# Gated attention and a max-out MLP on one core: other release points for the next sequence's loads of v

## The chip, the cores and the metric

The kernel runs on one core of one Trainium2 chip. The metric is the device time of one execution in microseconds (us), the median of several executions. Times inside an execution come from a profile of one execution and are counted from the start of its span.

## What is computed

There are eight sequences of 3072 tokens. u and v have 256 columns, z has 64, all float32.

```python
scores = scale * np.matmul(z, z.transpose(0, 2, 1))      # scale = 1/3072
attn = np.maximum(scores, 0.0) ** 2
x = u * np.matmul(attn, v)                               # then reshaped to 24576 x 256
h1, h2 = x @ w1, x @ w2                                  # 256 -> 1024
out = np.maximum(h1, h2) @ w_out                         # 1024 -> 256
```

The kernel computes in bfloat16 with float32 accumulation.

## The kernel before

**Steps.** A sequence is cut into six groups of 512 tokens (`G` = 4 blocks of 128 tokens, `NG` = 6 groups). A step computes the result of one group of queries; there are 48 steps, and step n belongs to sequence n // 6. The scores are symmetric, so a tile of scores of groups (i, j) is computed once, and its transpose is made by a DMA (`turn`, L564 for the diagonal blocks and `do_turn`, L449, for whole tiles, which land in tiles named aT). The product with v and the last layer are done by a scheme of seven products in place of eight of 2 x 2 blocks. This needs sums of blocks: VectorE makes sums of v's blocks once per pair of groups (`add_fold`, L366; the tile is called lf; the additions carry the lines L290 and L293), and sums of score blocks for each step (`add_sums`, L613; the tile es).

**Phases of a step.** From the fourth step on, TensorE goes through a step in four passes over the six groups: Xa and Xb (three products for each half) and Ya and Yb (four products for each half). Between and inside them stand the first layer of an earlier step (da, db), the last layer of a still earlier step (o), and the scores of steps to come. `QUIET` (L1483) holds the first job of Xb, of Ya and of Yb of each step: the beginnings of the second, third and fourth pass.

**Loads.** GpSimd issues all loads of u, v and z, since they cast float32 to bfloat16 (`load`, L107). Its queue is in order. A load of v (`add_v`, L344) brings one group, 512 tokens of 256 columns, 256 KB as bfloat16; the six groups come in the order 1, 2, 3, 4, 5, 0, and two of them in turn fill one tile and are folded together. The tile pool has six such tiles, so two sequences fit. Loads of the first sequence go out at the start. Any other load is timed: it waits for the newest matmul that stands ahead of it in the program (L109), so that it does not go out too early. u (`add_u`, L1497) is loaded one group for each step; z (`add_z`, L1525) is loaded for the next sequence in the third step, and its two transposes (zT) come after that. SyncE issues all transposes and stores, in order.

**Where a load is placed.** The place is given as a step of the sequence before and a time in us within that step by a plan of TensorE's work; `at_step` (L1479) finds the first job that the plan has at that time or later, and `quiet` (L1487) moves on to the next job of `QUIET`. For the sequences 2 to 7 (counted from 0) the loop at L1548 holds the list for v:

```python
            z_at, zT_at = (2, 9), (3, 4)
            v_at = [(3, 11), (3, 16), (4, 5), (4, 12), (5, 2), (5, 6)]
        add_z(b, quiet(at_step(b - 1, *z_at)), at_step(b - 1, *zT_at))
        for g, at in zip(v_order(b), v_at):
            add_v(b, g, quiet(at_step(b - 1, *at)))
```

Sequence 1 has a list of its own. u is placed at 4 us of a step, which `quiet` turns into the first job of Xb.

**The order of everything else.** The order on TensorE is written out beforehand (`pe_order`). A planner (`find_orders`, L1756) with costs of all jobs then decides the order on VectorE, ScalarE, SyncE and GpSimd, and which of ScalarE and VectorE does a job that either can do. A load's place enters this plan, and so do costs for DMAs. The orders are fixed in the program.

Of the kernel before, what the change touches and what calls it, by code (L numbers as in the profile page):

```python
# [11 lines left out]
def kernel(  # L12
# [306 lines left out]
    def v_order(b):  # L319
        return [1, 2, 3, 4, 5, 0] if b else list(range(NG))  # L320
# [23 lines left out]
    def add_v(b, g, at):  # L344
        first = v_pair(b, g)[1] == 0
        if first:
            buf(*v_key(b, g), lambda: vpool.tile([P, 2, G, D], bf16, name="v_sb"))

        def fetch(_):
            load(  # L350
                timed=at is not None,
                out=v_tile(b, g),
                in_=v[b].rearrange("(p t) d -> p t d", p=P)[:, ds(g * G, G), :],
            )

        job(
            ("v", b, g),
            {"POOL": 1300},
            fetch,
            new=v_key(b, g) if first else None,  # L360
            uses=[v_key(b, g)],
            after=list(at or ()) + ([] if first else [("v", b, v_order(b)[v_order(b).index(g) - 1])]),
            lag=8000,
        )
# [1114 lines left out]
    def at_step(b, s, us):  # L1479
        return pe_job_at(starts[NG * b + s] + us * 1000)  # L1480
# [6 lines left out]
    def quiet(at):  # L1487
        i = pe_order.index(at[0])
        if pe_at[i] < starts[LAG]:
            return at  # L1490
        found = [key for key in pe_order[i:] if key in QUIET]
        return found[:1] or at
# [32 lines left out]
    def add_z(b, at, turn_at):  # L1525
        def fetch(_):
            load(
                timed=True,
                out=z_sb_0[:, 1 : 1 + NSB, :],
                in_=z[b].rearrange("(p t) d -> p t d", p=P),  # L1530
            )

        def turn_z(_):
            seqs[b].zT = make_zT(z_sb_0)

        job(("z", b), {"POOL": 1800}, fetch, after=at, lag=7500)
        job(("zT", b), {"SP": 3500}, turn_z, deps=[("z", b)], after=turn_at, lag=3500)
# [10 lines left out]
    for b in range(1, B):  # L1548
        if b == 1:
            z_at, zT_at = (2, 6), (3, 2)  # L1550
            v_at = [(0, 8), (3, 12), (3, 16), (4, 4), (4, 8), (5, 4)]
        else:
            z_at, zT_at = (2, 9), (3, 4)
            v_at = [(3, 11), (3, 16), (4, 5), (4, 12), (5, 2), (5, 6)]
        add_z(b, quiet(at_step(b - 1, *z_at)), at_step(b - 1, *zT_at))
        for g, at in zip(v_order(b), v_at):
            add_v(b, g, quiet(at_step(b - 1, *at)))
# [422 lines left out]
```

## Time and profile before

| | us |
|---|---|
| runs shown | 908.16, 907.21, 898.59 |
| median | 907.21 |
| the profiled execution's own time | 907.36 |
| its span, first to last instruction | 905.6 |
| TensorE busy in the span | 887.9 |
| VectorE busy | 788.7 |
| ScalarE busy | 754.9 |
| GpSimd busy | 58.6 |
| median from issue to landing: v, u, a transpose to aT | 5.9, 5.4, 5.2 |

The span is 1.8 us shorter than the execution's own time. Busy time of an engine leaves out what its sequencer does (waits, issues of DMAs). A wait is put down to what ended it; "issue" means that the engine waited for nothing that the profile shows. "DMA share" is the time of all packets as a share of the 16 DMA engines' time; packets of several queues overlap, so that it can be over 1.

### The profile page before, as it was taken

The page shows a single profiled execution, that of the slowest core. Times are in us where ns is not written, and L with a number is a line of the kernel's source. Part 1 is how long each engine was busy: PE and PEld are TensorE (multiplying, and loading weights), DVE is VectorE, ACT ScalarE, POOL GpSimd, SP SyncE. Part 2 cuts the span into 40 slices and gives each one's busy share as a digit, 9 for nine tenths or more (in the row PEclk, how much of TensorE's full clock was granted, in tenths as well). Part 3 has the DMA queues.
Part 4 walks back from the last instruction along what each step waited for, and adds up shares of the span by engine and source line. Part 5 has one row for each costly group of instructions (what it writes and reads, how often), then busy time and mean ns, then how long its engine had stood idle before and what let it go on. Part 6 is the DMA issues. An engine that isn't in the chain of part 4 may idle for free.

```text
span 905.6 us, 37106 instructions
## 1 busy us (share of the span) xinstructions
PE 887.9 (98%) x16333; PEld 743.3 (82%) x16333; DVE 788.7 (87%) x1701; ACT 754.9 (83%) x946; POOL 58.6 (6%) x115
## 2 busy tenths in 40 slices
PE   8979999999999999999999989999999999999998
PEld 3349888988888888888888878888888898888885
DVE  6856888999999999999999889988999899989970
ACT  8846999789987899888997879977999789997635
POOL 3100000000000000001000000000000001000000
PEclk9989999999999999999999999999999999999999
DMA  9999999999999999999999999999999999999711
GB/s 164 188 136 178 173 183 158 188 155 180 172 166 151 171 184 156 162 175 188 156 159 171 186 151 150 166 173 165 184 149 182 164 190 160 158 172 159 124 61 70
DMA packets 382929, 146.64 MB, mean 162 GB/s; under 512 B 361264, under 2 KB 362928, under 8 KB 382768
## 3 DMA queue, kind: packets, MB, share of 16 engines
q1 hardware_dynamic: 366208, 114.54, 79.3%
q0 software_dynamic: 16560, 29.74, 23.4%
q8 instruction: 127, 2.08, 0.9%
q14 instruction: 34, 0.28, 0.1%
HBM read 59.77 MB, written 25.17 MB: 94 GB/s over the span
## 4 chain that ended last, share of the span: by engine, by line
PE 75%; DVE 12%; ACT 6%; DMA 3%; issue 3%; SPq 0%; POOL 0%; DVEq 0%; POOLq 0%
PE acc L87 38%; PE s_ps L87 37%; DVE es L290 2%; ACT g_sb L276 2%; DMA v_sb<-in_v_dram 2%; ACT a_sb L276 2%; DVE es L293 2%; DVE a_sb L293 1%; DVE e L290 1%; DVE xT L297 1%; DVE e L293 1%; DVE o_sb L293 1%; ACT a_sb L282 1%; DVE gs L293 1%; DMA z_sb<-in_z_dram 1%
## 5 line engine op out<-in xcount | busy, mean ns | idle before, releaser
L87 PEld LDWEIGHTS <-v_sb 64*128 64x128 bf16 (+1 forms) x4464 | 333.9, 94 | 68.3 <-issue 12.9
L276 ACT ACTIVATE a_sb<-s_ps 128x1024 bf16<-128x1024 f32 (+1 forms) x335 | 301.6, 944 | 36.3 <-PE s_ps L87 34.6
L87 PE MATMUL acc<-es,v_sb 64*128 64x256 bf16 x2160 | 278.5, 269 | 0.0
L87 PEld LDWEIGHTS <-lf 64*128 64x128 bf16 x3240 | 264.2, 94 | 17.2 <-POOLq L95 5.3
L87 PE MATMUL acc<-es,lf 64*128 64x256 bf16 x1080 | 246.6, 269 | 0.1
L87 PE MATMUL acc<-a_sb,lf 64*128 64x256 bf16 x1224 | 232.7, 269 | 0.0
L282 ACT ACTIVATE a_sb<-a_sb 128x1024 bf16<-128x1024 bf16 (+1 forms) x219 | 213.0, 993 | 2.3
L87 PE MATMUL s_ps<-xT,w_sb 64*128 64x512 bf16 (+1 forms) x1484 | 212.9, 376 | 0.1
L276 ACT ACTIVATE g_sb<-s_ps 128x1024 bf16<-128x1024 f32 x187 | 185.9, 1024 | 8.7 <-PE s_ps L87 7.2
L87 PE MATMUL acc<-aT,lf 64*128 64x256 bf16 x936 | 178.3, 269 | 0.9 <-issue 0.6
L87 PE MATMUL acc<-a_sb,v_sb 64*128 64x256 bf16 (+1 forms) x1344 | 142.4, 279 | 1.9 <-DMA a_sb<-a_sb 1.2
L87 PE MATMUL s_ps<-zT 64*128 64x512 bf16 (+2 forms) x774 | 120.2, 333 | 2.5 <-DVE o_sb L290 1.2
L290 DVE TENSOR_TENSOR es<-aT 128x1536 bf16<-128x1536 bf16 (+1 forms) x117 | 106.3, 930 | 0.0
L87 PEld LDWEIGHTS <-gs 64*128 64x128 bf16 x2688 | 98.7, 94 | 8.4
L87 PEld LDWEIGHTS <-g_sb 64*128 64x128 bf16 x2336 | 92.3, 94 | 11.9 <-POOLq L95 7.1
L87 PEld LDWEIGHTS <-w_sb 64*128 64x128 bf16 (+1 forms) x1488 | 79.5, 94 | 26.6 <-POOLq L95 1.0
L284 DVE TENSOR_TENSOR a_sb<-a_sb 128x1024 bf16<-128x1024 bf16 (+1 forms) x117 | 72.6, 625 | 23.7 <-ACT a_sb L276 23.5
L87 PE MATMUL acc<-aT,v_sb 64*128 64x256 bf16 x936 | 87.4, 270 | 3.5 <-DMA aT<-a_sb 3.5
L293 DVE TENSOR_TENSOR es<-a_sb 128x512 bf16<-128x512 bf16 x198 | 78.8, 418 | 6.7 <-PE acc L87 6.6
L87 PE MATMUL s_ps<-wf_sb,gs 64*128 64x128 bf16 x2016 | 80.8, 216 | 0.0
L87 PE MATMUL s_ps<-w_out_sb,g_sb 64*128 64x128 bf16 (+1 forms) x1664 | 79.7, 228 | 0.0
L290 DVE TENSOR_TENSOR es<-a_sb 128x1024 bf16<-128x1024 bf16 x108 | 72.0, 683 | 0.0
(87 smaller groups left out, 1079.5 us busy)
## 6 DMA issues: line engine op xcount, KB each, us to landing
out_dram<-o_sb SPq DMA_DIRECT2D x47, 512.0 KB, 4.7
v_sb<-in_v_dram POOLq DMA_DIRECT2D x48, 256.0 KB, 5.9
u_sb<-in_u_dram POOLq DMA_DIRECT2D x48, 256.0 KB, 5.4
aT<-a_sb SPq DMA_TRANSPOSE x228, 5.2
z_sb<-in_z_dram POOLq DMA_DIRECT2D x7, 384.0 KB, 6.8
w_sb<-in_moe_w_dram POOLq DMA_DIRECT2D x2, 512.0 KB, 7.6
uT<-u_sb SPq DMA_TRANSPOSE x48, 4.8
a_sb<-a_sb SPq DMA_TRANSPOSE x45, 5.3
```

The lines of the kernel that those rows point to most:

```text
L87: newest[0] = pin(nc.tensor.matmul(*args, **kw)).ins
L276: pin(nc.scalar.activation(out_ap, in_ap, AF.Relu))
L282: pin(nc.scalar.activation(ap, ap, AF.Square))
L284: pin(nc.vector.tensor_mul(ap, ap, ap))
L290: pin(nc.vector.tensor_add(*args))
L293: pin(nc.vector.tensor_sub(*args))
L297: nc.vector.scalar_tensor_tensor(out=out_ap, in0=in0, scalar=c2, in1=in1, op0=ALU.mult, op1=ALU.mult)
```

## The change

One line: for the sequences 2 to 7, the six loads of v get other places in the sequence before.

```diff
         else:
             z_at, zT_at = (2, 9), (3, 4)
-            v_at = [(3, 11), (3, 16), (4, 5), (4, 12), (5, 2), (5, 6)]
+            v_at = [(2, 13), (3, 9), (3, 13), (4, 9), (4, 13), (5, 9)]
         add_z(b, quiet(at_step(b - 1, *z_at)), at_step(b - 1, *zT_at))
         for g, at in zip(v_order(b), v_at):
             add_v(b, g, quiet(at_step(b - 1, *at)))
```

After `quiet`, the loads of v wait for these jobs of TensorE (steps counted from 0 within the sequence; u is loaded at the first job of Xb of each step, z at the first job of Ya of step 2):

| group | before | after |
|---|---|---|
| 1 | step 3, Yb | step 2, Yb |
| 2 | step 4, Xb | step 3, Ya |
| 3 | step 4, Xb | step 3, Yb |
| 4 | step 4, Yb | step 4, Ya |
| 5 | step 5, Xb | step 4, Yb |
| 0 | step 5, Ya | step 5, Ya |

The orders on TensorE, ScalarE and VectorE are the same in both programs. On GpSimd one place in each of the six sequences changes: group 1 comes ahead of the load of u that is issued in step 3. The loads of u issued in steps 4 and 5 keep their places behind groups 3 and 5. On SyncE two places in each of the six sequences change: during step 4 the transpose of u goes ahead of a store and of the transpose of a diagonal block, and during step 5 it and a store go ahead of the transpose of a tile of scores.

## The prediction

> **What bounds the kernel now.** I read the page first: its busy line, its forty slices and its DMA rows.
>
> ```profile
> span 905.6 us, 37106 instructions
> PE 887.9 (98%) x16333; PEld 743.3 (82%) x16333; DVE 788.7 (87%) x1701; ACT 754.9 (83%) x946; POOL 58.6 (6%) x115
> DMA  9999999999999999999999999999999999999711
> q0 software_dynamic: 16560, 29.74, 23.4%
> q8 instruction: 127, 2.08, 0.9%
> ```
>
> TensorE is busy for 98% of the span: 17.7 us are idle in all. The DMA engines are at 9 tenths or more in 37 slices of 40. So nothing that moves a load can win much unless a load now holds TensorE up, and any stretch with more loads in it may hurt. Next the windows of the six whole sequences whose loads the change moves (columns: stretch, its length, busy PE, PEld, DVE, ACT, POOL with counts, TensorE clock, DMA share, GB/s).
>
> ```profile
> 112.00:221.00 109.00, 108.84 (x2148) 94.74 (x2147) 98.27 (x211) 95.94 (x122) 6.37 (x12) 1.00 1.13 172
> 221.00:331.00 110.00, 107.63 (x2126) 93.63 (x2123) 101.16 (x221) 95.69 (x120) 6.90 (x13) 1.00 1.07 167
> 331.00:440.00 109.00, 108.80 (x2144) 94.48 (x2140) 101.95 (x222) 96.38 (x123) 6.90 (x13) 1.00 1.08 169
> 440.00:551.00 111.00, 107.45 (x2115) 93.75 (x2113) 101.10 (x220) 95.29 (x121) 6.90 (x13) 1.00 1.07 164
> ```
>
> Two sequences lose 2.37 us (110.00 − 107.63) and 3.55 us; the others, 551 to 769 us too, lose 0.2 each. The clock is 1.00 in all of them. TensorE's own waits from 112 to 770 us, in total, times, longest:
>
> ```profile
> PE s_ps L87 <- issue: 3.2, 2, 2.3
> PE s_ps L87 <- DVE o_sb L290: 1.2, 2, 0.6
> PE acc L87 <- DVE e L290: 0.6, 1, 0.6
> PE acc L87 <- issue: 0.6, 1, 0.6
> ```
>
> That is all there is to win: 5.6 us. None of it is a wait for a transposed tile or for v itself. I followed both kinds back.
>
> The waits for VectorE come from v. The chain of waits and VectorE's timeline have it: the last load of v of a sequence (group 0) lands late, the fold at L290 waits, and VectorE, busy without a break after that, is late for TensorE at 230.87 (0.62 us) and 243.57 (0.61 us), and at 462.22 (0.58 us).
>
> ```profile
> 221.37 6.84 DMA v_sb<-in_v_dram
> 440.93 5.94 DMA v_sb<-in_v_dram
> ```
> ```profile
> 228.34 0.42 DVE L290 TENSOR_TENSOR lf<-v_sb 128x512 bf16<-128x512 bf16 x1 [1.30 <-DMA v_sb<-in_v_dram]
> 446.99 0.43 DVE L290 TENSOR_TENSOR lf<-v_sb 128x512 bf16<-128x512 bf16 x1 [0.40 <-DMA v_sb<-in_v_dram]
> ```
>
> The waits for "issue" stand at 286.57 (0.98 us), 527.16 (0.60) and 542.87 (2.27). I read them as TensorE out of instructions: queue q8 moved 2.08 MB in 127 packets, 16.4 KB each, one for every 257 of PE's and PEld's 32,666 instructions. In the trace's packet records these three waits end 1.3 to 1.6 us after a q8 packet that began 12.2, 9.4 and 9.4 us behind the one before it, where the mean is 905.6/127 = 7.1. This is an inference. The timeline of GpSimd shows what was on the way just before the longest:
>
> ```profile
> 526.43 0.53 POOL L108 DMA_DIRECT2D v_sb<-in_v_dram  x1 [8.04 <-PE s_ps L87]
> 528.06 0.53 POOL L108 DMA_DIRECT2D v_sb<-in_v_dram  x1 [1.10 <-PE acc L87]
> 529.04 0.53 POOL L108 DMA_DIRECT2D u_sb<-in_u_dram  x1 [0.45 <-PE acc L87]
> 536.24 0.53 POOL L108 DMA_DIRECT2D v_sb<-in_v_dram  x1 [6.66 <-PE s_ps L87]
> ```
>
> Three loads within 2.6 us, then a fourth.
>
> **The change part by part.** Nothing is added or removed: 36 loads of v (six each for the third to the eighth sequence, groups in the order 1, 2, 3, 4, 5, 0) get other release points. Orders on TensorE, ScalarE and VectorE stay as they were; GpSimd's and SyncE's queues change. Each load waits for the newest matmul, so the new times are the ends of those matmuls in the trace of before. For the sequence loaded around 390 to 446 us (old → new): group 1 408.9 → 391.2; group 2 417.5 → 404.9; group 3 418.2 → 408.9; group 4 426.4 → 422.5; group 5 435.8 → 426.4; group 0 stays at 440.9. u, which has no load of v ahead of it for the same matmul any more, moves from 419.2 to 417.4 and from 436.7 to 435.8. z stays at 387.2.
>
> *Issue on GpSimd.* The same 0.53 us rows, on an engine 6% busy: nothing. Group 1 is now ahead of one u in the queue, but its matmul ends 8 us before that u's: no wait is inherited.
>
> *SyncE's queue.* Twice in each sequence a transpose of u moves ahead of a store and a transpose of scores; that blocks what stands behind it until u lands. Near 417 us u starts 1.8 us sooner, so its transpose can issue near 423 instead of 427.10; the store (issued at 423.73) hardly moves and the transpose of a diagonal block (420.89) goes some 3.6 us later, against 39 us until its first reader. Near 440 us a transpose goes from 439.64 to about 442.5; its tile is first touched again 28 us after it landed. Cost: nothing; the cover is these leads. Were they gone, the price would be the same 3 to 4 us on each.
>
> *Fold of the last pair.* Until now three loads (group 5, u, group 0) fall into the last 5 us before it, after the change two. Price of a load: q0's 23.4% of 905.6 us is 211.9 us for 29.74 MB, so 0.262 MB take 1.87 us of all engines. Group 0 lands up to 1.87 us sooner; VectorE waited 1.30 and 0.40. Both go. TensorE gets back 1.23 us, and of the 0.58 no more than the 0.40. Sum −1.6 (bounds 0 and −1.8).
>
> *The bunch of three.* Gone; loads come 4 to 9 us apart. The wait of 0.60 at 527 stays: it came with one load on the way, and group 3 takes group 1's old place. The 2.27 at 542.87 fell behind the bunch, but after the change groups 4 and 5 are near. I take −1.5, two thirds of it; the bounds are 0 and all three rows, −3.85.
>
> Here a page is weighed against these rows. The Trainium skill, "Runtime: NRT & Kernel Launch", section "Instruction fetch mechanics", says that instructions come in 16 KiB blocks of 256 and that this is mostly hidden. The size agrees (16.4 KB for 257 instructions); "hidden" would make these three waits something that no load changes, and this term zero.
>
> *z and group 1.* The third step gets a load more, 4 us behind z, where zT's transposes follow (396.56 to 401.35 on SyncE). The windows give a DMA share of 1.16 for 387 to 397 us, 1.33 for 397 to 407, against 1.00 for 417 to 427. Before the 0.98 us wait at 286.57 there was z alone (277 to 287 us: share 1.22). Group 1 can lengthen that, and start one in the other five sequences. Below: 0, since the other five show no wait there. Above: the largest row, 2.27, in each of six: +13.6. Nearest is the sequence that shows a wait: I take +0.8 in it (half of 2.27 − 0.98, and a little for the others).
>
> *Transposes behind it.* Everything on SyncE from 391 to 411 us shares its time with one load more, and the last transposes there with two: up to 2 × 1.87 = 3.7 us later. The tightest tile there, the fourth step's turned group 4, lands at 410.46 and TensorE reads it 4.19 us later (4.3 to 6.4 in the other sequences); zT has 6.4. Cost: nothing by 0.5 us; if all fails, about 1 us in each of six.
>
> Sum: −1.6 − 1.5 + 0.8 = −2.3. The profiled execution took 907.36 us (span 905.6 and 1.8 around it), 0.15 above the median of 907.21. 907.36 − 2.3 − 0.15 = 904.9.
>
> **The rivals.**
> *All stalls go.* If bunches caused every issue wait, the whole 5.6 us goes: 907.2 − 5.6 = 901.6. For it: the undisturbed sequences lose only 0.2 us, and one of the three runs took 898.59, so TensorE's work fits into that. Against: two of the three issue waits had one load beside them. Its range runs from 898 to 902, and lower only if the runs lose something that this execution doesn't show.
> *Loads don't reach the issue waits.* Only the fold's term is left: 907.2 − 1.6 = 905.6. For it: v's bunch stands in all six sequences and only one shows the long wait. This is what the page above, the Trainium skill's "Instruction fetch mechanics", would make of it.
> *Slower: group 1 behind z starves TensorE in every sequence.* Place: 391 to 407 us and its like. Price: 2.27 each, 13.6 − 1.6 = +12.0: 919.2. For it: the highest DMA shares, and the one wait there with z alone. Against: five of six showed none. It decides from (9.1 + 1.6)/6 = 1.8 us a sequence on; at 0.98 it is 911.5 and within 1%.
>
> **How the numbers follow.** A measurement can tell about 1% from no change here: 9.1 us, so 898.1 and 916.3. The forecast, 901 to 911, has 0.45; all stalls gone 0.27; loads without effect on issue 0.09; starved 0.19. Under 898.1 lies about half of the second case at most: 0.14. Over 916.3 the fourth: 0.19. Within: 0.67. The time is that of the forecast. The range leaves out the fourth case and takes in the second to its end: 897.5 to 912.
>
> **What would show it.** Right: no wait for DMA ahead of any fold at L290 in the third to eighth sequence; TensorE's waits for VectorE under 0.5 us; issue waits of 2 to 3 us in all, the larger ones 5 to 20 us behind z. Wrong: issue waits in most sequences, or TensorE waiting for aT in the fifth step; or a sum of issue waits that hasn't moved though the loads stand apart.

## The result, and the profile after

The changed kernel took 908.77 us (median of 20 executions, 903.49 to 918.14), the kernel before 904.07 (20 executions, 898.59 to 908.16). The ratio is 1.0049, with a 95% interval of 1.003 to 1.0068: slower by about 4.4 us, half of the 1% that the prediction took for no change, but clear of chance. Ratios here and below leave out the few slow executions (here the one of 918.14 us), and so differ a little from the quotient of the medians. The forecast was 904.9 and a gain of a quarter of a per cent: the direction is wrong. That the forecast lies within 4 us of the median is in part luck. It was counted down from 907.21, the median of three executions; counted from the 904.07 of twenty, the same sum gives 901.8.

The profiled execution after took 912.19 us. Its page, busy line first:

```profile
span 910.4 us, 37107 instructions
PE 889.9 (98%) x16333; PEld 744.7 (82%) x16333; DVE 788.6 (87%) x1701; ACT 754.7 (83%) x946; POOL 58.4 (6%) x115
```

The span is 4.8 us longer: TensorE is idle for 2.8 us more (20.5 in place of 17.7) and busy for 2.0 more. The work of VectorE and ScalarE is the same. The same windows as before (stretch, length, busy PE, PEld, DVE, ACT, POOL, clock, DMA share, GB/s):

```profile
112.00:221.00 109.00, 107.97 (x2124) 93.72 (x2121) 98.02 (x211) 95.54 (x121) 6.34 (x12) 1.00 1.08 170
221.00:331.00 110.00, 109.11 (x2158) 94.69 (x2154) 101.86 (x222) 96.31 (x122) 6.87 (x13) 1.00 1.08 169
331.00:440.00 109.00, 108.72 (x2146) 94.53 (x2142) 102.03 (x222) 96.51 (x122) 6.88 (x13) 1.00 1.08 170
440.00:551.00 111.00, 104.97 (x2056) 91.37 (x2054) 98.27 (x217) 92.30 (x116) 6.34 (x12) 1.00 1.16 159
...
660.00:769.00 109.00, 107.97 (x2125) 93.72 (x2123) 100.98 (x222) 95.35 (x121) 6.86 (x13) 1.00 1.08 169
```

The stretch from 440 to 551 us now loses 6.03 us (111.00 − 104.97), where it lost 3.55. The first, the second and the last lose about 1 each; the other two lose 0.3. In the second, 221 to 331 us, this is less than the 2.37 of before: the issue wait of 0.98 us that the prediction expected to grow is not there. TensorE's own waits from 112 to 770 us (in total, times, longest):

```profile
PE s_ps L87 <- issue: 4.6, 3, 2.1
PE acc L87 <- DMA aT<-a_sb: 1.5, 1, 1.5
PE acc L87 <- issue: 1.5, 3, 0.7
PE s_ps L87 <- ACT a_sb L282: 0.5, 1, 0.5
PE s_ps L87 <- DVE o_sb L290: 0.2, 1, 0.2
```

They sum to 8.3 us, where they were 5.6. The waits for VectorE have shrunk from 1.8 to 0.2; "issue" has grown from 3.8 to 6.1, and a wait for a turned tile (aT) is there that was not. Where they stand is seen in two timelines of the changed kernel. GpSimd:

```profile
496.10 0.53 POOL L108 DMA_DIRECT2D z_sb<-in_z_dram  x1 [4.50 <-PE acc L87]
500.03 0.53 POOL L108 DMA_DIRECT2D v_sb<-in_v_dram  x1 [3.40 <-PE s_ps L87]
510.96 0.53 POOL L108 DMA_DIRECT2D u_sb<-in_u_dram  x1 [10.40 <-PE s_ps L87]
```

And TensorE:

```profile
509.79 0.38 PE L87 MATMUL s_ps<-wf_sb,gs 64*128 64x128 bf16 x7 [2.08 <-issue]
...
524.95 0.27 PE L87 MATMUL s_ps<-w_out_sb,g_sb 64*128 64x128 bf16 x3 [1.66 <-issue]
...
529.50 0.28 PE L87 MATMUL acc<-aT,lf 64*128 64x256 bf16 x2 [1.49 <-DMA aT<-a_sb]
```

Group 1 of v (500.03) follows z by 3.9 us, and in the 30 us behind it TensorE loses 5.2 us. SyncE's queue shows the jam. Before (start, us on SyncE's queue):

```profile
499.32 2.85 SPq L104 DMA_TRANSPOSE aT<-a_sb  x1
...
504.67 4.80 SPq L104 DMA_TRANSPOSE zT<-z_sb  x2
...
510.89 1.45 SPq L104 DMA_TRANSPOSE aT<-a_sb  x1
```

After:

```profile
499.04 7.66 SPq L104 DMA_TRANSPOSE aT<-a_sb  x1
...
510.21 8.47 SPq L104 DMA_TRANSPOSE zT<-z_sb  x2
...
521.90 2.28 SPq L104 DMA_TRANSPOSE aT<-a_sb  x1
```

The jobs at 499 us and zT held SyncE for 16.13 us in place of 7.65, and the transposes behind them came late. The last line of each is the tile aT for which TensorE waits at 529.50: it goes out 11 us later than before. The median time from issue to landing went from 6.8 to 7.5 us for z and from 6.1 to 7.1 for its transposes.

**What an "issue" wait is.** The prediction took it for a wait for instructions, and that can be put to the trace: if instructions come in blocks of 256, such a wait can stand only at one place of a block, where those at hand run out. Counting PE's and PEld's instructions from the start of the program, modulo 256, at the first matmul behind every issue wait over 0.15 us between 100 and 800 us gives:

```
before                     3 waits at 186 186 187
after                      6 waits at 183 185 185 186 187 187
the ten experiments below  28 waits, all at 183 to 190
TensorE's other waits      46, spread from 35 to 231
```

All 37 issue waits of the first three rows fall within eight neighbouring counts of 256, and each ends 1.3 to 2.8 us after the end of a 16 KB packet of the instruction queue (35 of them 1.3 to 1.6). It is sharper still when the 15 instructions of TensorE's that are neither a matmul nor a weight load are counted too: when TensorE goes on and k packets have landed, it stands at instruction 256 k + 193 or 256 k + 195, in all 37 cases. That is as direct as a trace can be: TensorE has used up what had come, and goes on with the packet that has just landed.

### The profile page after: what moved, and what is told of

Same layout as the page of the kernel before. It is cut to its first block, busy times and chain, and to the rows that moved or that the text cites. A ratio compares the mean times of both kernels' runs of the same rounds, so it can differ in the third digit from the quotient of the medians.

```text
span 910.4 us, 37107 instructions
## 1 busy us (share of the span) xinstructions
PE 889.9 (98%) x16333; PEld 744.7 (82%) x16333; DVE 788.6 (87%) x1701; ACT 754.7 (83%) x946; POOL 58.4 (6%) x115
## 4 chain that ended last, share of the span: by engine, by line
PE 74%; DVE 13%; ACT 7%; issue 3%; DMA 2%; SPq 0%; POOL 0%; POOLq 0%; DVEq 0%
PE acc L87 37%; PE s_ps L87 37%; ACT a_sb L276 3%; ACT g_sb L276 3%; DVE es L290 2%; DVE es L293 2%; DVE a_sb L293 1%; ACT a_sb L282 1%; DVE e L290 1%; DVE xT L297 1%; DVE o_sb L293 1%; DVE e L293 1%; DMA aT<-a_sb 1%; DVE gs L293 1%; DMA v_sb<-in_v_dram 1%
## 5 line engine op out<-in xcount | busy, mean ns | idle before, releaser
L87 PEld LDWEIGHTS <-g_sb 64*128 64x128 bf16 x2336 | 93.3, 95 | 13.3 <-POOLq L95 7.1
```

The lines of the kernel that those rows point to most:

```text
L87: newest[0] = pin(nc.tensor.matmul(*args, **kw)).ins
```

## The experiments

Ratios are to the kernel before, in alternating executions on the same chip, with 95% intervals. Four theories were set against each other: A, group 1 costs because it stands beside z and what follows it; B, the loads 4 to 5 us apart make one long train in the fourth and fifth step; C, SyncE's other order costs; D, an earlier group 1 costs wherever it is put. The orders on TensorE, ScalarE and VectorE are those of before in every kernel.

**Group 1 alone.** On the kernel before:

```diff
-            v_at = [(3, 11), (3, 16), (4, 5), (4, 12), (5, 2), (5, 6)]
+            v_at = [(2, 13), (3, 16), (4, 5), (4, 12), (5, 2), (5, 6)]
```

> The kernel before, with group 1 alone moved to its new place (third step, Yb, 4 us behind z); SyncE's order is that of before. Theory A (group 1 beside z and the transposes of z is what costs): the whole loss of the change or more, 0.4 to 0.9% slower than before, with issue waits of TensorE in the third and fourth step. Theory B (u, v and v dealt 4 to 5 us apart make one long train of loads in the fourth and fifth step): no change, within 0.2%. Theory C (SyncE's other order costs): no change, within 0.2%.

Measured: 1.0058 (1.0028 to 1.0088), as slow as the whole change. TensorE's issue waits in its profile, all within 30 us behind group 1:

```profile
PE acc L87 <- issue: 1.8, 2, 1.5
PE s_ps L87 <- issue: 1.0, 1, 1.0
```

A holds: the place of group 1 makes the loss. B and C fall: neither the train nor SyncE's other order is in this kernel. How the 5 us come about is only in part seen here. In this one profiled execution TensorE's waits from 112 to 770 us sum to 5.0 us, against 5.6 before, and from the matmul that stands at 112 us to the last one it takes 0.1 us less than the execution before. What does show in each of the six sequences is the jam: the first of z's two transposes takes 7.0 to 13.2 us from issue to landing, where it took 5.4 to 7.0.

**All but group 1.** On the changed kernel, group 1 goes out with group 2:

```diff
-            v_at = [(2, 13), (3, 9), (3, 13), (4, 9), (4, 13), (5, 9)]
+            v_at = [(3, 9), (3, 9), (3, 13), (4, 9), (4, 13), (5, 9)]
```

> The changed kernel, with group 1 no longer behind z: it goes out together with group 2 at the first job of Ya of the fourth step. SyncE's order is that of the changed kernel. Theory A: back to the time of before or 0.1 to 0.3% below it, since the bunch of three is gone too. Theories B and C: still about 0.5% slower than before.

Measured: 1.0017 (0.9991 to 1.0043): not told from before. So the rest of the change costs little, if anything, and no gain is seen either, though the bunch of three is gone.

**z a step earlier.** On the changed kernel:

```diff
-            z_at, zT_at = (2, 9), (3, 4)
+            z_at, zT_at = (1, 9), (3, 4)
```

> The changed kernel, with the load of z moved a step earlier (second step, Ya), so that group 1 has no load of z just ahead of it; the transposes of z stay where they were in the plan. Theory A, if the two loads side by side cost: back to the time of before, within 0.2%. Theory A, if the load of v costs because it falls among the transposes: still 0.3 to 0.6% slower. Theories B and C: still about 0.5% slower.

Measured: 1.0015 (0.9984 to 1.0046). Group 1 is where the change has it, and z's transposes have the same place in SyncE's order (one store goes out a place earlier). The load of z has left, and the loss of half a per cent is no longer seen. In time, the transposes of z are even nearer to group 1 than in the changed kernel: 2.4 us behind it in the sequence loaded from 388 us, where they were 6.8 us behind. So a load of v near the transposes is not enough; it is the two loads side by side, with the transposes behind them. This rests on one run whose interval still reaches 1.0046.

**A quarter of v.** On the changed kernel, loads of the third to eighth sequence bring one block of four (and reuse the tile of two sequences before):

```diff
-            buf(*v_key(b, g), lambda: vpool.tile([P, 2, G, D], bf16, name="v_sb"))
+            old = ("v", (b - 2, v_pair(b, g)[0]))
+            buf(*v_key(b, g), lambda: vpool.tile([P, 2, G, D], bf16, name="v_sb") if b < 2 else tile_of(*old))
 
         def fetch(_):
+            part = G if b < 2 else 1
             load(
                 timed=at is not None,
-                out=v_tile(b, g),
-                in_=v[b].rearrange("(p t) d -> p t d", p=P)[:, ds(g * G, G), :],
+                out=v_tile(b, g)[:, :part, :],
+                in_=v[b].rearrange("(p t) d -> p t d", p=P)[:, ds(g * G, part), :],
```

> The changed kernel, with three quarters of v left out for the third to eighth sequence: every load of v there brings one block of 128 tokens in place of four, into the tile of the sequence two before, so that the rest is old data. Places and orders stay. If loads of v are what delays TensorE's instructions (A or B): issue waits between 112 and 770 us fall from 6.1 us to under 2, and the time goes 0.3 to 0.8% below that of before. If the issue waits have nothing to do with the loads (the order on SyncE, C, or something else): still about 0.5% slower than before.

Measured: 0.9974 (0.9941 to 1.0007). Its profile has no wait of TensorE from 112 to 770 us at all; the window:

```profile
112.00:770.00 658.00, 656.85 (x12962) 571.31 (x12959) 616.67 (x1340) 583.25 (x735) 41.23 (x78) 1.00 1.01 160
```

What is lost is 1.2 us in 658. Its interval lies wholly below that of the changed kernel, so the loads' bytes are behind the loss. That they are behind the issue waits is what this one profiled execution speaks for. It also suggests how little any placing of v could win over before: with three quarters of the bytes gone the gain is some 0.3%, 0.6% at the interval's end, and not clear of 1.

**Group 1 elsewhere.** On the kernel before, group 1 at the second step's Yb, where no z is near:

```diff
-            v_at = [(3, 11), (3, 16), (4, 5), (4, 12), (5, 2), (5, 6)]
+            v_at = [(1, 13), (3, 16), (4, 5), (4, 12), (5, 2), (5, 6)]
```

> The kernel before, with group 1 alone moved, but a step earlier than the change moves it: second step, Yb, where no load of z is near. Theory A (it costs because it is beside the load of z and what follows it): within 0.25% of before. Theory D (it costs wherever it stands in a step that had u alone until now): 0.4 to 0.6% slower, as with group 1 behind z.

Measured: 0.9979 (0.9958 to 1.0001). D falls: the same load, moved further still, costs nothing there. Since the interval only just reaches 1, it ran a second time:

> The kernel before with group 1 alone at the second step's Yb, a second time, since the first gave a ratio of 0.9979 with an interval that just reaches 1. If that was real: 0.1 to 0.4% faster again. If it was chance: within 0.2% on either side.

Measured: 0.9987 (0.9954 to 1.002). Twice on the same side, neither clear of 1: by the ratios a gain of 0.1 to 0.2%, not shown. Both intervals lie below that of group 1 behind z (1.0028 to 1.0088).

**The change with group 1 a step earlier.**

```diff
-            v_at = [(2, 13), (3, 9), (3, 13), (4, 9), (4, 13), (5, 9)]
+            v_at = [(1, 13), (3, 9), (3, 13), (4, 9), (4, 13), (5, 9)]
```

> The changed kernel, with group 1 a step earlier (second step, Yb); all else, SyncE's order too, as in the changed kernel. Theory A: within 0.25% of before, and if the bunch of three was worth something, up to 0.3% below it. Theory D: still about 0.5% slower than before.

Measured: 1.0012 (0.9981 to 1.0042). One slot moved, and the loss of the whole change is no longer seen; every load of v and z now stands alone, without a gain that is seen. This interval and that of the change overlap a little; but the three kernels in which the changed kernel loses the pair of z and group 1 (1.0017, 1.0015 and 1.0012) all lie below the change's interval.

**The cost doubled, here and there.** A second load of the same size behind group 1; once in the changed kernel, once in the last one:

```diff
+            if b >= 2 and g == 1:
+                load(timed=True, out=v_tile(b, 2), in_=v[b].rearrange("(p t) d -> p t d", p=P)[:, ds(2 * G, G), :])
```

> The changed kernel, with the suspected cost doubled: right behind group 1 a second load of the same size (group 2's data, into the place that group 2's own load fills again later), for the third to eighth sequence. Theory A: 0.9 to 1.6% slower than before, with issue waits or waits for aT in the third and fourth step of several sequences. Theory D: about as slow as the same extra load a step earlier.

> The changed kernel with group 1 a step earlier and the same extra load behind it there: as many bytes as with the extra load behind z, away from z. Theory A: 0 to 0.4% slower than before, at least 0.5% faster than the extra load behind z. Theory D: as slow as the extra load behind z.

Measured: 1.0226 (1.0176 to 1.0277) behind z, 1.0062 (1.0033 to 1.009) a step earlier. The same bytes cost 1.6% more behind z, which is A. The first was worse than foreseen. TensorE's waits from 112 to 790 us in its profiled execution, which at 933.91 us is the slowest of the six that were timed:

```profile
PE acc L87 <- issue: 9.6, 3, 4.8
PE acc L87 <- DMA aT<-a_sb: 7.5, 4, 3.2
PE s_ps L87 <- issue: 3.7, 3, 2.0
PE s_ps L87 <- ACT e L809: 2.1, 1, 2.1
```

Two loads behind z cost 2.3%, one 0.5%: the price goes up faster than the bytes. Part of it is the clock. At the three longest of these waits (4.84, 3.23 and 3.87 us) the granted clock falls to half for a while (columns as above, the clock third from the end):

```profile
189.20:192.60 3.40, 2.86 (x22) 2.06 (x24) 0.00 (x0) 0.09 (x1) 0.00 (x0) 0.50 1.35 142
428.20:435.00 6.80, 5.85 (x78) 5.23 (x79) 3.15 (x6) 3.33 (x6) 0.53 (x1) 0.50 1.21 223
639.80:646.60 6.80, 5.74 (x63) 4.72 (x65) 0.64 (x2) 1.24 (x3) 0.00 (x0) 0.50 1.17 149
```

TensorE is busy for 896.9 us in this execution, 9.0 more than before, of a span that is 26.5 longer. And away from z a third load in one step is not free either (0.6%, above the 0 to 0.4% of the expectation). There TensorE's longest waits are for turned tiles, 7.7 us in all from 112 to 770 us, against 4.2 of issue waits.

**z earlier in the kernel before.** The edit of z above, on the kernel before:

> The kernel before, with the load of z a step earlier (second step, Ya) and the loads of v where they were: every load of v or z away from the transposes of z, but the bunch of three stays. Theory A: the issue wait that before shows beside z goes, at most 0.3% faster; within 0.2% is as likely. If the bunch of three is what makes the issue waits of before: no change.

Measured: 1.0000 (0.9965 to 1.0035), with 0.2 us of issue waits from 112 to 770 us in its profile. No version tried beats the kernel before by more than its interval.

**What one profile can't tell.** Issue waits from 112 to 770 us sum to 6.1, 2.8, 4.2 and 13.3 us in the profiles of the slower kernels (the change, group 1 alone, the extra load a step earlier and behind z). In those that are not slower they sum to 3.8 (before) and 2.7, 1.3, 2.0, 1.0, 0.2 and 2.7 (all but group 1, z a step earlier, group 1 elsewhere, the change with group 1 a step earlier, z earlier in the kernel before, group 1 elsewhere again). The last is a single wait of 2.74 us, 11 us behind z with no load of v near. So the ratios show that the place of group 1 costs 0.5 to 0.6%; that the cost goes by late instructions and late transposes is seen where they stand, but a single profile doesn't add up to it.

## Why the prediction was wrong, step by step

*What bounds the kernel, and what can be won.* Right. TensorE is never far from full, and emptying the loads by three quarters wins some 0.3%, not clear of chance.

*The issue waits are instructions that come late because of loads.* Right that they are late instructions, and now shown: all 37 stand at one place of a block of 256. That loads make them late rests on less: none with a quarter of v and 13.3 us with the extra load behind z, but between 0.2 and 3.8 in kernels of the same time. The weighing against the Trainium skill, "Runtime: NRT & Kernel Launch", section "Instruction fetch mechanics", came out on the side of the rows. Its blocks of 256 instructions are in the trace to the count; that crossing one is mostly hidden is so for most of the 127, and in the profiles of before and after the rest are the largest of TensorE's waits (3.8 of 5.6 us and 6.1 of 8.3).

*The bunch of three: −1.5.* Not borne out. Without the bunch, and with group 1 out of z's way, the ratio is 1.0012 or 1.0017. The two terms of gain together, −3.1 us or 0.9966, lie below both intervals; −1.5 alone, 0.9983, lies just inside the first (0.9981 to 1.0042). One 2.27 us wait in one profiled execution was taken for a cost of the place. The two readings that the prediction held against it were the better ones: the bunch stands in six sequences and only one showed the wait, and a lone load had one too.

*z and group 1: +0.8.* The step that failed, in size: the mechanism and the place were written down, with the stretch of highest DMA share, and priced for the one sequence that already showed a wait. Measured by itself it is 0.58% of 902.19, 5.2 us, or 0.9 on average in each of six sequences. The prediction took 0.8 for all six together. With 5.2 its sum is −1.6 − 1.5 + 5.2 = +2.1: this term alone turns the sign. Taking the row of 0.98 us for every sequence would have given 5.9. That five sequences showed no wait there in one execution was read as room, and was none: in the profile after, the sequence that was priced shows no issue wait, and three others do.

*The fold of the last pair: −1.6.* The sign is right in the changed kernel's profile: the fold goes on without a wait,

```profile
228.74 0.42 DVE L290 TENSOR_TENSOR lf<-v_sb 128x512 bf16<-128x512 bf16 x1
```

and TensorE's waits for VectorE fall from 1.8 to 0.2 us. But with groups 5 and 0 at the same places, the kernel with all but group 1 has two such waits for v in its profile, 1.6 us in all. The wait comes and goes from one execution to the next, and no experiment shows a gain in the time.

*Transposes behind it: nothing.* Wrong by one wait. Up to 3.7 us of delay were set against 4.19 of lead; in the sequence in which SyncE's queue was held 8.5 us longer, the tile that the prediction named as the tightest goes out 11 us later and costs 1.49 us. The delay was counted from the bytes of the loads, and SyncE's queue, which holds up all that stands behind, was left out. With the extra load there are four such waits, 7.5 us.

*GpSimd's issue and SyncE's order: nothing.* Right as far as can be told: group 1 alone, with SyncE's order of before, has the whole loss.

*The rivals.* "Starved behind z" was the mechanism, at under half of the price given and not in every sequence (three issue waits of 0.4 to 1.5 us in the profile of group 1 alone). It stood with a chance of 0.19, at the price of the largest row; at the 0.98 row, by the prediction's own figure, it gives 911.5, slower than before. "All stalls go" falls with the two spread versions. "Loads don't reach the issue waits" would leave a gain of 1.6 us, and the change is slower; the quarter of v speaks against it too.

## What to carry to other kernels

A load put into a stretch in which the DMA queues are near full is priced by what stands behind it there, instructions included, and the price is to be counted for all repetitions, even if one profile shows a wait in only some of them. Before moving loads for even spacing, look which of the new places is already the fullest, and move that one load elsewhere; here that decides 0.5%, and for the even spacing itself no gain was seen. One wait of 2 us in one profiled execution is no term of a sum until it is seen at the same place in the other repetitions.

## What the runs showed of the hardware

The first 70 us, which no kernel here changes, differ by several us between executions. TensorE's granted clock from 30 to 68 us in the profiles of before, of a quarter of v and of z earlier (PE busy and count, then the others, clock, DMA share, GB/s):

```profile
30.00:68.00 38.00, 32.99 (x223) 15.97 (x223) 25.07 (x50) 23.98 (x28) 2.02 (x3) 0.91 1.20 157
```
```profile
30.00:68.00 38.00, 37.53 (x316) 20.44 (x315) 28.20 (x57) 28.36 (x34) 2.63 (x5) 1.00 1.19 181
```
```profile
30.00:68.00 38.00, 30.55 (x175) 12.85 (x174) 20.98 (x40) 23.92 (x28) 2.01 (x3) 0.93 1.26 140
```

In the same 38 us the matmuls done run from 175 to 316. The step that follows begins 72.4 us into the profiled execution before and 67.4 in that with a quarter of v. That is as much as the whole effect of the change. In the execution before, TensorE waits 3.45 us there for a turned tile (until 61.34), and its clock is at half from 60.1 to 66.9 us; in that with a quarter of v it has neither. Why that wait comes in some executions only stays open. Behind 112 us single executions differ too, as that of group 1 alone showed. So single executions can't be compared here, only medians over many.

The fall of the clock can be followed through all twelve traces. Behind 100 us they hold six waits of TensorE longer than 2.5 us (2.68, 2.74, 3.23, 3.60, 3.87 and 4.84), and during each of them or within 1.2 us of its end the granted clock falls to half, for 3.4 or 6.8 us. At the 20 waits of 1.0 to 2.3 us it stays at 1.00. In the first 70 us it falls at a shorter one too (1.79 us, in group 1 elsewhere). So a long wait costs TensorE more than its own length.

And TensorE's instructions come through the DMA engines like the data: 127 packets of 16 KB for 32,666 instructions, one every 7.1 us. When one comes late, TensorE stops without any wait that the program has written.
